# A gated feed-forward after windowed attention: w_gate's products in block form too, with PSUM banks taken in pairs

## The chip, the core and the metric

The kernel runs on one core of one Trainium2 chip. A core has a matrix engine (TensorE, here PE, with its weight loads PEld), three engines for everything else (VectorE or DVE, ScalarE or ACT, GpSimd or POOL), a queue that issues DMAs (SyncE or SP; POOL issues DMAs too), an on-chip memory SBUF and the accumulators PSUM, eight banks of 128 partitions by 512 float32. Each engine runs its instructions in order and waits on semaphores for the others. The metric is the device time of one execution in microseconds (us). Three timed runs of the kernel before gave 322.5, 322.76 and 321.5; the median is 322.5.

## The reference

Inputs are q, k, v of (8 batches, 8 heads, 576 positions, 64), and three weight matrices; everything is given as float32.

```python
scores = scale * q @ k.T            # only the 64 last positions of each query count
attn   = softmax(scores) ; x = (attn @ v) as (4608 tokens, 512)
gate   = maximum(x @ w_gate, 0)     # 512 x 1536
val    = x @ w_val                  # 512 x 1536
out    = (gate * val) @ w_out       # 1536 x 512
```

## The kernel before, in words

The tokens are cut into ten tiles: four narrow ones of 384 tokens (tiles 0 to 3) and six wide ones of 512 (tiles 4 to 9). For each tile x is made transposed in SBUF (`xt`: 512 features as 4 blocks of 128 partitions, by tokens), then a stage called hidden makes `g_sb = relu(x w_gate) * (x w_val)`, 12 blocks of 128 columns, and a stage called output multiplies it by w_out, 128 tokens at a time, copies each result from PSUM (`o_sb`, on ACT) and stores it (SP). Everything in the matmuls is float16, the accumulation float32.

Attention for later tiles is woven into these stages. `scores` (wide) and `u_st` (narrow) compute scores into PSUM, ACT takes exp, DVE masks; `values` multiplies by v, DVE divides by the sums (L436, L441) and transposes the result into `xt` (L447). q and k come by DMA (L173, issued by POOL, one buffer for each of four halves) and are transposed by DVE (L193, 1.24 us each, 32 in all); v comes by DMA (L199) and is spread to a second place by POOL (`v_spread`, L208 and L210).

**Order.** `W`, the Weaver, keeps a planned clock and a heap of due times. PE's instructions are emitted in the order of the code; each emission first pops all other work whose due time has come, so the order on every engine is fixed when the program is built. `W.pop()` in a loop emits work early until something (a free bank, a sum) is there. `plan_batch` plans the loads and transposes of one batch of q and k, `qk_ahead` gives it the time of the load (12 us ahead of T) and of the four transposes; `v_ahead` does it for v.

**Banks.** `singles` are eight PSUM tiles of one bank each. In the narrow tiles `one_bank` goes round the first four and `two_banks` round the other four. From the first wide tile on, `free` lists banks not in use; `bank()` takes the oldest, and the reader of a bank appends it again.

**Hidden of a narrow tile** (`hidden`, L507 to L545): in sets of four blocks, first the four products with w_gate, each into a bank, with a relu by ACT into one slot of `r4` (L522), then four with w_val, each multiplied by its relu by DVE straight from PSUM into `g_sb` (L525).

**Hidden of a wide tile** (`fast_hidden`, L547 to L642): three groups. Each covers two blocks of the first half of the columns and two of the second. w_val's part is done with seven products of half-size blocks instead of eight (a Strassen-like scheme). P1 to P7 are products of sums of weight blocks (`vs`, made once by POOL in `w_form`, L480) with differences of x blocks (`xc`, four for each tile, made by DVE in `x_form`, L459). P1, P6, P7 and P4 run up in one bank, A: after P1, P6 and P7 ACT copies the running sum out (`snap`, L593), and the next product is added on top. P2 goes to bank B; P5 and P3 to bank C. DVE adds B or C to a copy (L600), and POOL multiplies that sum by its relu into `g_sb` (L606); the last one, P4's, DVE multiplies straight from PSUM (`direct`, L613). Between these products stand the four full products with w_gate (`gate`, 4 matmuls of 512 columns each, L582), each with a relu by ACT from PSUM (L586).

**Output of a wide tile** (`fast_output`): four rows of 128 tokens, 12 matmuls of 512 columns each (L658); ahead of the first two stand the values of the next tile, ahead of the last two the scores of the one after.

Of the kernel before, what the change touches and what calls it, by code (L numbers as in the profile page):

```python
# [15 lines left out]
SUB = mybir.AluOpType.subtract  # L16
ONE_ONE = struct.unpack("<f", struct.pack("<I", 0x3C003C00))[0]
# [29 lines left out]
def kernel(  # L47
# [23 lines left out]
    WT = 512  # L71
# [15 lines left out]
    singles = [psum.tile([128, 512], FP32, name=f"bank{i}") for i in range(8)]  # L87
# [7 lines left out]
    vs = persist.tile([128, 4, 2, 128 * HF], FP16)  # L95
    qTs = [persist.tile([128, 2, S, 2], FP16, name=f"qT{i}") for i in range(2)]
# [266 lines left out]

    def bank():

        while not free:
            W.pop()
        return free.pop(0)
# [83 lines left out]
    def x_form(t, n):  # L452

        if t not in xcs:
            xcs[t] = x_sb.tile([128, 4, 2, HT], FP16, name="xc", tag="xt")
        xt, xc = xt_tile(t), xcs[t]
        b11, b12, b21, b22 = (xt[:, 2 * k:2 * k + 2, HT * h:HT * h + HT] for k in range(2) for h in range(2))
        x, y = ((b12, b11), (b22, xc[:, 0]), (b22, b12), (b21, xc[:, 1]))[n]
        nc.vector.tensor_tensor(xc[:, n], x, y, SUB)  # L459
        if n == 3:  # L460
            normed[0] = t

    def values(t, hh, T, banks=None):
# [7 lines left out]
        for n in ((0,), (1, 2, 3))[hh]:  # L471
            W.at(T + 4.0 + 0.4 * n, lambda n=n: x_form(t, n))

    def w_form(n, j):

        c = slice(256 * j, 256 * j + 256)
        f = slice(256 * j + 128 * HF, 256 * j + 128 * HF + 256)
        a11, a12, a21, a22 = wv[:, 0:2, c], wv[:, 2:4, c], wv[:, 0:2, f], wv[:, 2:4, f]
        x, y, op = ((a21, a22, ADD), (vs[:, 0, :, c], a11, SUB), (a11, a21, SUB), (a12, vs[:, 1, :, c], SUB))[n]
        nc.gpsimd.tensor_tensor(vs[:, n, :, c], x, y, op)  # L480
# [26 lines left out]
    def hidden(t, spans, f0=0, f1=NF, each=1):  # L507
# [20 lines left out]
        for fb in range(f0, f1, each):  # L528
            r4 = f_sb.tile([128, 4, WT], FP32, name="r4", bufs=2)
            r_sbs = {}  # L530
            for i, wt in enumerate((wg, wv)):
                for c0, f in ((c0, f) for c0, _ in spans for f in range(fb, fb + each, w)):
# [8 lines left out]
                    if i == 0:  # L541
                        r_sb = r_sbs[c0, f] = r4[:, len(r_sbs)]
# [4 lines left out]
    def fast_hidden(t):  # L547
# [3 lines left out]
        b11, b12, b21, b22 = (xt[:, 2 * k:2 * k + 2, HT * h:HT * h + HT] for k in range(2) for h in range(2))  # L551
        halves = lambda ap: ap.rearrange("p f (h n) -> p f h n", h=2)
        pair = lambda ap: ap.rearrange("p (f n) -> p f n", f=2)

        def group(j):
            c = slice(256 * j, 256 * j + 256)
            f = slice(256 * j + 128 * HF, 256 * j + 128 * HF + 256)
            r4 = f_sb.tile([128, 4, WT], FP32, name="r4", bufs=2)
            rh = halves(r4)
            gh = halves(g_sb)  # L560
            at = {}
            forms = {"P1": (wv[:, 0:2, c], b11), "P2": (wv[:, 2:4, c], b21), "P3": (vs[:, 3, :, c], b22),
                     "P4": (wv[:, 2:4, f], xc[:, 3]), "P5": (vs[:, 0, :, c], xc[:, 0]),
                     "P6": (vs[:, 1, :, c], xc[:, 1]), "P7": (vs[:, 2, :, c], xc[:, 2])}

            def product(name, to, first):
                W.advance(W.clock)
                if first:
                    at[to] = bank()
                w, x = forms[name]  # L570
                for i in range(2):
                    for k in range(2):
                        nc.tensor.matmul(at[to][:, HT * i:HT * i + HT], w[:, k, 128 * i:128 * i + 128], x[:, k],  # L573
                                         start=(first and i == 0 and k == 0), stop=(k == 1), skip_group_check=True)
                W.clock += 4 * (HT + 7) / 2400.0

            def gate(n):
                W.advance(W.clock)
                to = bank()
                ff = 2 * j + n % 2 + HF * (n // 2)  # L580
                for k in range(NC):
                    nc.tensor.matmul(to, wg[:, k, 128 * ff:128 * ff + 128], xt[:, k], start=(k == 0), stop=(k == NC - 1))  # L582
                W.clock += 4 * (WT + 7) / 2400.0

                def relu():
                    nc.scalar.activation(r4[:, n], to, ACT.Relu)  # L586
                    free.append(to)
                W.at(W.clock, relu)

            def snap(name):  # L590
                def copy():
                    at[name] = f_sb.tile([128, 512], FP32, name="snap", bufs=5)
                    nc.scalar.copy(at[name], at["A"])  # L593
                W.at(W.clock, copy)

            def add(delay, to, name, last, n, h):

                def summed():
                    v = f_sb.tile([128, 512], FP32, name="vsum", bufs=4)
                    nc.vector.tensor_tensor(v, at[to], at[name], ADD)  # L600
                    at["summed", n, h] = True
                    if last:
                        free.append(at[to])

                    def mult():
                        nc.gpsimd.tensor_tensor(gh[:, 2 * j + HF * n:2 * j + HF * n + 2, h], rh[:, 2 * n:2 * n + 2, h], pair(v), MUL)  # L606
                        done[2 * j + HF * n, h] = done[2 * j + HF * n + 1, h] = True
                    W.at(max(W.clock, at["relus", n]) + 0.7, mult)
                W.at(W.clock + delay, summed)

            def direct():
                def mult():
                    nc.vector.tensor_tensor(gh[:, 2 * j + HF:2 * j + HF + 2, 0], rh[:, 2:4, 0], pair(at["A"]), MUL)  # L613
                    free.append(at["A"])
                    done[2 * j + HF, 0] = done[2 * j + HF + 1, 0] = True
                W.at(W.clock + 0.2, mult)

            T = W.clock
            at["relus", 1], at["relus", 0] = T + 3.7, T + 6.8
            product("P1", "A", True)  # L620
            snap("a1")
            gate(2)
            product("P6", "A", False)
            snap("u2")
            product("P2", "B", True)
            add(0.1, "B", "a1", True, 0, 0)
            gate(3)
            product("P5", "C", True)
            product("P7", "A", False)
            snap("u3")  # L630
            add(0.8, "C", "u3", False, 1, 1)
            gate(0)
            product("P4", "A", False)
            direct()
            gate(1)
            while ("summed", 1, 1) not in at:
                W.pop()
            product("P3", "C", False)
            add(0.1, "C", "u2", True, 0, 1)

        for j in range(NF // 4):
            group(j)  # L642
# [76 lines left out]
    with tc.manual_schedule():  # L719
# [115 lines left out]
        def qk_ahead(t, T, gaps):  # L835
            b, new = batch_of(t)
            if new:
                plan_batch(b, T - 12.0, [T + x for x in gaps])
# [13 lines left out]
        def ahead(t):  # L852
# [3 lines left out]
            if t == NS - 2:  # L856
                qk_ahead(NS, T + 20.5, (0.0, 1.5, 3.0, 4.5))
                v_ahead(NS, T + 27.0)
                for j in range(NF // 4):
                    for n, at in enumerate((0, 1, 3, 2)):  # L860
                        W.at(T + 12.0 + 6.4 * j + 1.6 * n, lambda at=at, j=j: w_form(at, j))
            if t == NS - 1:
# [9 lines left out]
                qk_ahead(NS + 2, T + 27.6, SLOTS)  # L872
# [7 lines left out]
        W.at(15.0, lambda: loads(3, 70.0))  # L880
        T = 67.0
# [65 lines left out]
```

## Time and profile before

| | |
|---|---|
| timed runs, median (range) | 322.5 us (321.5 to 322.76) |
| profiled execution, span from first to last instruction | 320.2 us |
| mean granted PE clock | 0.995 |
| one wide tile, hidden and output (223.09 to 256.0) | 32.9 us, of which hidden 19.6 |
| busy in a wide tile's hidden stage without q/k transposes (256.0 to 275.5): PE, DVE, ACT, POOL | 19.5, 7.4, 12.3, 8.6 us |
| the same with four q/k transposes (190.2 to 209.7) | 19.5, 12.0, 12.3, 13.0 us |

No time of the profiled execution as a whole is recorded besides its span; the timed runs lie 1.3 to 2.6 us above it. In the rows of the profile, "x" is a count, "busy, mean ns" the time of a group and of one instruction, and after the bar stands the idle time of the engine just before them and what ended it. A matmul's row gives a modelled end, which includes the way through the array; matmuls that follow each other start earlier than the row before ends.

### The profile page before, as it was taken

To read this page: it belongs to the slowest core of one execution; us is meant where nothing else is said; L and a number is where in the kernel's file an instruction comes from. 1 tells how busy PE (TensorE), PEld (TensorE's weight loads), DVE (VectorE), ACT (ScalarE), POOL (GpSimd) and SP (SyncE) were. 2 spreads that over 40 slices of the span, in tenths; PEclk is the share of its full clock that TensorE was granted. 3 is DMA by queue.
4 is the path that set the end of the run, shared out by engine and by line. 5 is a ranking of instruction groups with operands and counts; after the bars stand their busy time and mean duration, and the time that the engine had idled before them with its cause. 6 is when DMAs were issued, how large, how long until landed. Compare 5 with 4: busy or idle time off the path is not lost.

```text
span 320.2 us, 9481 instructions
## 1 busy us (share of the span) xinstructions
PE 308.8 (96%) x4077; PEld 190.1 (59%) x4077; DVE 203.2 (63%) x397; ACT 158.1 (49%) x310; POOL 177.8 (56%) x206
## 2 busy tenths in 40 slices
PE   4799999999899999999999999999999999999996
PEld 2586958655546555665566556655665566546654
DVE  6937962667993996779576857686337734643420
ACT  3644325533524616752765276627652666326632
POOL 8859336215988506799168925980495036404540
PEclk9889999999999999999999999999999999999999
DMA  8999998946299149806910691039001100020002
GB/s 218 183 196 205 194 120 161 171 98 99 30 174 165 21 90 160 57 1 104 219 36 0 97 220 43 2 50 127 35 0 34 69 34 3 2 98 35 0 33 102
DMA packets 52491, 29.52 MB, mean 92 GB/s; under 512 B 38880, under 2 KB 43872, under 8 KB 52448
## 3 DMA queue, kind: packets, MB, share of 16 engines
q0 software_dynamic: 46688, 18.29, 49.3%
q1 hardware_dynamic: 5616, 10.55, 9.3%
q8 instruction: 32, 0.52, 0.7%
q14 instruction: 11, 0.09, 0.1%
q10 hardware_dynamic: 144, 0.07, 0.1%
HBM read 37.75 MB, written 9.44 MB: 147 GB/s over the span
## 4 chain that ended last, share of the span: by engine, by line
PE 89%; DVE 3%; ACT 2%; POOL 2%; DMA 2%; issue 1%; DVEq 0%; POOLq 0%
PE bank L658 19%; PE bank L582 19%; PE bank L538 17%; PE bank L573 17%; PE bank L673 10%; PE bank L253 3%; PE bank L422 2%; DVE p L292 2%; DMA v<-in_v_dram 2%; ACT pw L389 1%; PE bank L311 1%; DVE g_sb L525 1%; PE bank L703 1%; POOL v L199 1%; DVE qT L193 0%
## 5 line engine op out<-in xcount | busy, mean ns | idle before, releaser
L606 POOL TENSOR_TENSOR g_sb<-r,vsum 128x512 f16<-128x512 f32 x54 | 68.1, 1276 | 77.7 <-DVE vsum L600 75.7
L600 DVE TENSOR_TENSOR vsum<-bank,snap 128x512 f32<-128x512 f32 x54 | 37.3, 691 | 60.1 <-PE bank L573 36.5
L582 PE MATMUL bank<-xt,wg 128*128 128x512 f16 x288 | 73.9, 379 | 0.0
L658 PE MATMUL bank<-wo,g_sb 128*128 128x512 f16 x276 | 62.9, 380 | 0.0
L586 ACT ACTIVATE r<-bank 128x512 f32<-128x512 f32 x72 | 43.2, 600 | 32.3 <-PE bank L582 32.3
L658 PEld LDWEIGHTS <-g_sb 128*128 128x128 f16 x276 | 25.5, 98 | 28.9
L582 PEld LDWEIGHTS <-wg 128*128 128x128 f16 x288 | 28.2, 98 | 18.6
L525 DVE TENSOR_TENSOR g_sb<-r,bank 128x384 f16<-128x384 f32 x48 | 25.9, 550 | 20.3 <-PE bank L538 18.8
L522 ACT ACTIVATE r<-bank 128x384 f32<-128x384 f32 x48 | 23.7, 496 | 29.4 <-PE bank L538 20.3
L573 PEld LDWEIGHTS <-vs 128*128 128x128 f16 x288 | 28.0, 98 | 15.6 <-issue 1.6
L538 PE MATMUL bank<-xt,wg 128*128 128x192 f16 (+1 forms) x256 | 36.5, 296 | 0.5 <-DVE g_sb L525 0.4
L663 ACT COPY o_sb<-bank 128x512 f32<-128x512 f32 x23 | 13.5, 586 | 45.2 <-PE bank L658 43.2
L593 ACT COPY snap<-bank 128x512 f32<-128x512 f32 x54 | 31.6, 586 | 8.4 <-PE bank L573 8.4
L199 POOL DMA_DIRECT2D v<-in_v_dram x41 | 34.7, 865 | 1.8 <-DMA q<-in_q_dram 1.0
L538 PE MATMUL bank<-xt,wv 128*128 128x192 f16 (+1 forms) x256 | 34.3, 286 | 0.0
L673 PE MATMUL bank<-wo,g_sb 128*128 128x512 f16 x144 | 32.8, 379 | 0.2 <-DVE g_sb L525 0.2
L538 PEld LDWEIGHTS <-wg 128*128 128x128 f16 x256 | 24.3, 102 | 9.8 <-issue 0.9
L573 PE MATMUL bank<-xc,vs 128*128 128x256 f16 x216 | 29.4, 272 | 0.4 <-ACT snap L593 0.4
L208 POOL COPY v<-v 64x512 f16<-64x512 f16 (+1 forms) x22 | 16.1, 732 | 23.7 <-DMA v<-in_v_dram 22.6
L538 PEld LDWEIGHTS <-wv 128*128 128x128 f16 x256 | 22.9, 98 | 8.1
L394 DVE TENSOR_TENSOR pw<-pw,mask 128x512 f16<-128x512 f16 x48 | 20.2, 437 | 11.2 <-ACT pw L389 10.5
L389 ACT ACTIVATE pw<-bank 128x512 f16<-128x512 f32 x48 | 25.9, 608 | 1.5 <-PE bank L253 1.0
(69 smaller groups left out, 358.6 us busy)
## 6 DMA issues: line engine op xcount, KB each, us to landing
out_dram<-o_sb SPq DMA_DIRECT2D x35, 256.0 KB, 3.0
k<-in_k_dram POOLq DMA_DIRECT2D x15, 288.0 KB, 5.3
q<-in_q_dram POOLq DMA_DIRECT2D x15, 288.0 KB, 7.3
v<-in_v_dram POOLq DMA_DIRECT2D x31, 128.0 KB, 8.0
wg<-in_moe_w_gate_dram POOLq DMA_DIRECT2D x6, 256.0 KB, 6.4
wv<-in_moe_w_val_dram POOLq DMA_DIRECT2D x6, 256.0 KB, 8.2
wo<-in_moe_w_out_dram POOLq DMA_DIRECT2D x3, 512.0 KB, 11.9
v<-in_v_dram POOLq DMA_DIRECT2D x10, 64.0 KB, 5.9
```

What stands on the lines that cost most here:

```text
L199: nc.gpsimd.dma_start(v16s[b % 2][lo:hi, g, :, 0:64], v[b, :, 64 * g - 64 + lo:64 * g - 64 + hi].rearrange("h p d -> p h d"))
L389: nc.scalar.activation(d["p"][g].rearrange("p n c -> p (n c)"), d["st"][g], ACT.Exp, scale=scale)
L525: nc.vector.tensor_tensor(g_sb[:, f:f + w, c0:c0 + n], part(r_sb), part(h2), MUL)
L538: nc.tensor.matmul(h[:, b * n:b * n + n], wt[:, c, (f + b) * 128:(f + b) * 128 + 128], xt[:, c, c0:c0 + n], start=(c == 0), stop=(c == NC ...
L573: nc.tensor.matmul(at[to][:, HT * i:HT * i + HT], w[:, k, 128 * i:128 * i + 128], x[:, k], start=(first and i == 0 and k == 0), stop=(k == ...
L582: nc.tensor.matmul(to, wg[:, k, 128 * ff:128 * ff + 128], xt[:, k], start=(k == 0), stop=(k == NC - 1))
L586: nc.scalar.activation(r4[:, n], to, ACT.Relu)
L593: nc.scalar.copy(at[name], at["A"])
L600: nc.vector.tensor_tensor(v, at[to], at[name], ADD)
L606: nc.gpsimd.tensor_tensor(gh[:, 2 * j + HF * n:2 * j + HF * n + 2, h], rh[:, 2 * n:2 * n + 2, h], pair(v), MUL)
L658: nc.tensor.matmul(op, g_sb[:, f, 128 * sub:128 * sub + 128], wo[:, f], start=(i == 0), stop=(i == NF - 1))
L673: nc.tensor.matmul(op, g_sb[:, f, bass.ds(sub * 128, 128)], wo[:, f], start=(f == 0), stop=(f == NF - 1))
```

## The change: w_gate also in seven block products

The six wide tiles compute w_gate's part in the same seven-product form as w_val's. The two run side by side: each product is emitted for w_gate (i = 0) and then for w_val (i = 1). Bank A becomes two banks, one for each, B and C become pairs of neighbouring banks. The eight PSUM tiles are declared as four tiles of two banks, and `singles` are views of their halves. The copies of A go into the two halves of an SBUF tile `pr`; one DVE addition over 1024 columns adds both banks of B (or of C, the second time) to it; after P7 there are two additions of 512, since C goes on being used. ACT then takes the relu of the gate half in SBUF, and POOL multiplies the two halves. `bank()` prefers a bank whose neighbour is in use, and `bank_pair()` takes two neighbours. The first product of the next group is put between P4 and P3. POOL makes weight sums `us` of w_gate, 12 more instructions, planned from 42 us on; three of the four x differences of each tile go from DVE to POOL. One batch of q and k is loaded 6 us before its time instead of 12. The narrow tiles keep their computation; they use the new bank views, and `pr` pairs in place of `r4`.

```diff
-    singles = [psum.tile([128, 512], FP32, name=f"bank{i}") for i in range(8)]
+    pairs = [psum.tile([128, 2, 512], FP32, name=f"bank{i}") for i in range(4)]
+    singles = [pairs[i // 2][:, i % 2] for i in range(8)]
...
+    us = persist.tile([128, 4, 2, 128 * HF], FP16)
...
     def bank():
         while not free:
             W.pop()
-        return free.pop(0)
+        return take(next((to for to in free if not is_free(partner(to))), free[0]))
+
+    def bank_pair():
+        while True:
+            for to in free:
+                if is_free(partner(to)):
+                    i = next(i for i in range(8) if singles[i] is to) // 2
+                    return pairs[i], [take(singles[2 * i]), take(singles[2 * i + 1])]
+            W.pop()
...
-        nc.vector.tensor_tensor(xc[:, n], x, y, SUB)
+        (nc.vector if n == 1 else nc.gpsimd).tensor_tensor(xc[:, n], x, y, SUB)
...
-        for n in ((0,), (1, 2, 3))[hh]:
-            W.at(T + 4.0 + 0.4 * n, lambda n=n: x_form(t, n))
+        for n, x in (((0, 4.0),), ((1, 4.0), (2, 4.1), (3, 5.0)))[hh]:
+            W.at(T + x, lambda n=n: x_form(t, n))
...
-            r4 = f_sb.tile([128, 4, WT], FP32, name="r4", bufs=2)
+            r2s = [f_sb.tile([128, 2, WT], FP32, name="pr", bufs=6) for _ in range(2)]
...
+        TO = {"P1": "A", "P6": "A", "P7": "A", "P4": "A", "P2": "B", "P5": "C", "P3": "C"}
+        AFTER = {"P6": ("P1", "snap"), "P7": ("P6", "snap"), "P4": ("P7", "snap"), "P3": ("P7", "sum")}
+
+        def product(j, name, i):
+            W.advance(W.clock)
+            if name in AFTER:
+                before, what = AFTER[name]
+                while (j, what, before, i) not in at:
+                    W.pop()
+            first = name in ("P1", "P2", "P5")
+            if name == "P1":
+                at[j, "A", i] = bank()
+            elif first and i == 0:
+                at[j, TO[name]], (at[j, TO[name], 0], at[j, TO[name], 1]) = bank_pair()
+            to = at[j, TO[name], i]
+            w, x = operands(name, *kinds[i], j)
+            for m in range(2):
+                for k in range(2):
+                    nc.tensor.matmul(to[:, HT * m:HT * m + HT], w[:, k, 128 * m:128 * m + 128], x[:, k],
+                                     start=(first and m == 0 and k == 0), stop=(k == 1), skip_group_check=True)
+            W.clock += 4 * (HT + 7) / 2400.0
...
+            def copy():                                   # in snap(j, name, i)
+                nc.scalar.copy(pr[:, i], at[j, "A", i])
...
+            def relu():                                   # in finish(j, name, n, h)
+                nc.scalar.activation(pr[:, 0], pr[:, 0], ACT.Relu)
+            def mult():
+                nc.gpsimd.tensor_tensor(gh[:, f:f + 2, h], pair(pr[:, 0]), pair(pr[:, 1]), MUL)
...
+                if i is None:                             # in add(...)
+                    flat = [ap.rearrange("p a n -> p (a n)") for ap in (at[j, bank_name], pr)]
+                    nc.vector.tensor_tensor(flat[1], flat[0], flat[1], ADD)
+                    free.extend(at[j, bank_name, m] for m in range(2))
+                else:
+                    nc.vector.tensor_tensor(pr[:, i], at[j, bank_name, i], pr[:, i], ADD)
...
+        step(0, "P1")
+        for j in range(last + 1):
+            for name in ("P2", "P6", "P5", "P7") if j == 0 else ("P6", "P2", "P7", "P5"):
+                step(j, name)
+            tail = [(j, "P4"), (j + 1, "P1"), (j, "P3")] if j else [(j + 1, "P1"), (j, "P4"), (j, "P3")]
+            for jj, name in tail:
+                if jj <= last:
+                    step(jj, name)
...
-                qk_ahead(NS + 2, T + 27.6, SLOTS)
+                qk_ahead(NS + 2, T + 27.6, SLOTS, 6.0)
...
+        for j in range(NF // 4):
+            for n, at in enumerate((0, 1, 3, 2)):
+                W.at(42.0 + 8.8 * j + 2.2 * n, lambda at=at, j=j: w_form(wg, at, j))
```

In `step`, each of the two products of a name is followed by its `snap` (P1, P6, P7), and the additions, the relu of P4's gate bank and DVE's direct multiply are planned behind them as before.

## The prediction

> **What bounds the kernel now.** I read the page's first two parts, then the chain that ended last, then the costliest groups, then the timeline of one wide tile.
>
> ```profile
> span 320.2 us, 9481 instructions
> PE 308.8 (96%) x4077; PEld 190.1 (59%) x4077; DVE 203.2 (63%) x397; ACT 158.1 (49%) x310; POOL 177.8 (56%) x206
> ...
> PE 89%; DVE 3%; ACT 2%; POOL 2%; DMA 2%; issue 1%; DVEq 0%; POOLq 0%
> ...
> L582 PE MATMUL bank<-xt,wg 128*128 128x512 f16 x288 | 73.9, 379 | 0.0
> L586 ACT ACTIVATE r<-bank 128x512 f32<-128x512 f32 x72 | 43.2, 600 | 32.3 <-PE bank L582 32.3
> L525 DVE TENSOR_TENSOR g_sb<-r,bank 128x384 f16<-128x384 f32 x48 | 25.9, 550 | 20.3 <-PE bank L538 18.8
> L522 ACT ACTIVATE r<-bank 128x384 f32<-128x384 f32 x48 | 23.7, 496 | 29.4 <-PE bank L538 20.3
> L593 ACT COPY snap<-bank 128x512 f32<-128x512 f32 x54 | 31.6, 586 | 8.4 <-PE bank L573 8.4
> ```
>
> PE is busy for 96% and carries 89% of the chain. Its matmul groups have 0.0 to 0.5 us of idle time ahead of them; ACT and DVE idle, and PE is what releases them. So time falls only with PE's issue time, and grows with each wait put in front of PE. The timeline of the fourth wide tile shows how those waits stand today (start, length, engine, line).
>
> ```profile
> 223.03 0.49 PE L573 MATMUL bank<-xt,wv 128*128 128x256 f16 x3
> 223.16 0.59 ACT L663 COPY o_sb<-bank 128x512 f32<-128x512 f32 x1 [0.66 <-ACT pw L389]
> ...
> 223.65 0.59 ACT L593 COPY snap<-bank 128x512 f32<-128x512 f32 x1
> ...
> 224.29 0.60 PE L573 MATMUL bank<-xc,vs 128*128 128x256 f16 x4
> ...
> 226.02 1.04 PE L573 MATMUL bank<-xc,vs 128*128 128x256 f16 x8
> ...
> 226.90 1.03 PE L582 MATMUL bank<-xt,wg 128*128 128x512 f16 x4
> 227.10 0.59 ACT L593 COPY snap<-bank 128x512 f32<-128x512 f32 x1 [0.28 <-PE bank L573]
> ...
> 227.78 0.69 DVE L600 TENSOR_TENSOR vsum<-bank,snap 128x512 f32<-128x512 f32 x1 [1.63 <-ACT snap L593]
> ```
>
> Eight 256-column matmuls start at 226.02 and PE's next group at 226.90 (0.108 us each, so a block product of four issues in 0.433). Their modelled end is 227.06, 0.17 after the issue ends; the copy starts 0.04 later. The copy of 223.65 ends at 224.24 and the product that waited for it starts at 224.29, 0.05 later. Now a 0.86 us gate product lies in that gap; the wait costs 0.07.
>
> **The change, part by part.**
>
> *The products.* A group of a wide tile has 16 matmuls of 512 columns (0.216 us: four in 0.86, "226.90" to the next) and 28 of 256; after, 56 of 256. 16 x 0.216 + 28 x 0.108 = 6.49, against 56 x 0.108 = 6.07. That is 0.42 less, 1.27 for a tile's three groups, 7.6 for six tiles, if nothing waits.
>
> *The banks.* PSUM's eight tiles of one bank become four of two banks, and all code, narrow tiles too, uses halves of them. In the built program I counted out whose completion each PE wait names. P6 with wv writes the second half of a pair, and its wait is not for the copy of its own half. It is for the copy of the *other* half, which was issued just after P6 with wg:
>
> ```
> L606 Matmult bank1_83<-xc_2922,us_90 128x256 [waits Activation_49]   P6, wg: waits for the copy of P1's wv half
> L606 Matmult bank1_83<-xc_2922,vs_89 128x256 [waits Activation_49]   P6, wv: waits for the copy of P6's wg half
> ```
>
> So a pair is guarded as one tile: whoever writes a half waits for the last reader of either. With the products of w_gate and w_val alternating in the two halves of pair A, the wv product always waits out a full round trip that the wg product has just begun; and PE, in order, holds everything behind it (its own other products, and through them ACT and DVE, which idle).
>
> Price of a round trip: 0.17 drain + 0.05 + reader + 0.05. Reader 0.59 (a copy): 0.86. Relu of 384 (0.496): 0.76. Gate multiply of 384 (0.55): 0.82. Bounds: 0.76 for the first if the copy counts with its back-to-back spacing (o_sb at 223.16, snap at 223.65: 0.49), 0.96 if ACT is late by another 0.1.
>
> Wide tile, from the list of waits:
> - P1, P6, P7, P4 with wv, three groups: 12 x 0.86 = 10.3. A wait for the wg copy stands at each; P4's is for the relu.
> - The tile's first P1 takes the other half of the pair that held the last output row: 0.86 for the copy to o_sb.
> - The third group's P1 pair is the second group's P4 pair. DVE's direct multiply reads its wv half and is itself put behind P1 with wg, and the copy of that P1 behind the multiply: 0.17 + 0.05 + 0.69 + 0.05 + 0.59 + 0.05 = 1.60 instead of 0.86: 0.75 more.
>
> 12.0, less 1.3 for the products: hidden goes from 19.6 (223.09 to 242.69) to 30.3. Six tiles: **+64**.
>
> Narrow tiles: 24 bank fills each, 96 in all. Every second fill is the second half of its pair; the list shows 24 of them behind the relu of the half filled just before and 22 behind its gate multiply: 24 x 0.76 + 22 x 0.82 = **+36**. Before, each fill had a bank of its own, and L538's groups waited 0.5 and 0.0.
>
> Output rows: a row in the half beside the row before waits for its copy to o_sb. With two narrow fills that do the same these are 11 x 0.86 = 9.5; two first rows wait for a gate multiply, 1.6. In five wide tiles the first output row shares a pair with a values bank and waits for DVE to normalise it, some 0.9 each, 4.7 (0 if DVE is early, 1.4 each if its queue is full). **+16**, less some 1 us of PE waits of before that are contained in these.
>
> *The other edits, hidden.* ACT gets three operations more per group (six copies, four relus, against three and four): 54 x 0.6 = 32 us. With 6.07 us of PE per group it would be tight (10 starts of 0.49); with 10.3 it is covered by PE's own waits. DVE: two sums of 1024 and two of 512 for three of 512. No row has 1024 from PSUM; L525 to L600 grows 0.141 us in 128 columns, so 0.69 + 0.56 = 1.25, bounds 1.1 (no second fixed part) and 1.38 (two of 512): +1.8 a group, 33 us, less 18 differences at 0.42 to 0.52. Behind those sums wait the relus, the products P3 and the GpSimd multiplies; all have over 1 us of slack in a group of 10. Without that cover see rival C. GpSimd: 12 weight sums at 1.16 (L480's rows) and 18 differences, nearest row the same, 1.2. The first five weight sums lie in its idle stretch before 45.4 (9.7 us); three stand ahead of the k/q DMA issues of 48.4 and delay them by 3.6, three more ahead of the v issues of 50.5 (7.2 in all), one in the idle 8.8 before 62.05. The k/q transposes start at 66.65 and the v copies are wanted at 86, so landing times of 5.3 to 8.0 leave room. The differences stand behind the four k/q loads and ahead of the v loads; they end before the next tile's P6, since some 9 us of output rows lie between. The four loads issued 6 us later still land (5.3 and 7.3) before their transposes. All 0; ends -1 and +3.
>
> Sum: 64 + 36 + 15 = +115. The profiled execution's span is 320.2, the median of the timed runs 322.5, 2.3 around it; so a span of 435.5, and **438**.
>
> **A rule weighed.** The Trainium skill ("PSUM — Partial Sum Buffer", PSUM bank collisions) asks for guards by bank, and says different banks don't collide; by it the waits between halves are needless and the sum would be rival C's. The built program has them all the same, and it is what runs.
>
> **Rivals.**
>
> *B, the clock falls as well.* The granted clock was 0.63 from 13.8 to 18.4 us, right after 5.5 us in which PE was busy for only 3.86, and 1.00 once PE had run without gaps:
>
> ```profile
> 8.30:13.80 5.50, 3.86 (x196) 2.56 (x196) 5.12 (x12) 3.78 (x16) 3.93 (x7) 1.00 1.71 175
> 13.80:18.40 4.60, 4.46 (x34) 4.05 (x33) 2.23 (x6) 2.69 (x9) 4.60 (x7) 0.63 1.24 204
> 18.40:22.40 4.00, 4.00 (x43) 3.48 (x42) 2.22 (x4) 1.00 (x3) 1.65 (x3) 1.00 1.53 191
> ```
>
> After the change PE issues for some 60% of a wide hidden stage and 63% of a narrow one. At 0.63 the narrow ones' 96 x 0.64 (four matmuls of 384; sixteen took 2.76) = 61 us of issue grow by 36 (474), the wide ones' 6 x 18.2 by another 64 (538). Against it: that stretch was the start, with products of 64 columns; no gap now would exceed 1.9 us. The Trainium skill ("TensorE: Matmul & The Clock Gate", Part 1: The HAM clock gate) has the clock fall after an idle window of some 3.4 us, by which it would hold here; no row shows a warm PE with such gaps.
>
> *C, halves guarded apart.* Then copies end 0.44 us before their next product (0.43 + 0.17 + 0.05 + 0.59 + 0.05 = 1.29 of 1.73). What remains per tile is 0.43 for the first P1 and 0.74 for the third group's P1 behind relu and direct multiply, against 1.34 gained: -0.2. In the three tiles with q/k transposes (1.24 each) among DVE's sums, the direct multiply comes 1.5 later and P3 0.8: +2.2. 3 x 2.2 - 3 x 0.2 = +6: 328. Against it stands the counted list.
>
> *D, not slower.* As C, and DVE's transposes fall into its idle time: 322.5 - 7.6 = 315, up to 322. One wait decides: PE's for the wg half's copy at the wv product. It would have to be under 0.11 us (7.6 over the 72 of them); the round trip is 0.86.
>
> **How the numbers follow.** As worked out 0.72, B 0.20, C 0.05, D 0.03. The likeliest's own range: about 150 waits at 0.1 less or more, 424 to 453. The range must take in half of B: 424 to 500. Less than 0.5% (1.6 us) can't be told from no change here: faster 0.02, same 0.01, slower 0.97.
>
> **What would show it.** PE's busy share falls to some 70%, and PE leads the list of waits: on ACT's copies some 50 us, on ACT's and DVE's work of the narrow tiles 18 each, on the wide relu 15. A wide hidden stage lasts 30 us, its wv products start 0.86 after the wg product's issue ended. PEclk stays 9 (B: falls to 6). Copies at L617 idle before them for PE, not the reverse. Wrong if a wide tile's hidden stage stays under 25, or if PE's idle time before L562 is small.

## The result

The changed kernel takes 441.04 us (median of 4 runs, 439.74 to 443.1), the kernel before 322.0 (321.46 to 322.76): a ratio of 1.370, 95% interval 1.365 to 1.374. It is 119 us slower, where +115 and 438 were predicted. The profiled execution's span is 438.4 us at a granted clock of 0.992, against 320.2 at 0.995.

The page of the kernel after: span and busy times, the rows of TensorE and its clock by slices, the chain that ended last, and three of the costliest groups.

```profile
span 438.4 us, 9997 instructions
PE 324.0 (74%) x4293; PEld 211.1 (48%) x4293; DVE 240.3 (55%) x397; ACT 187.3 (43%) x364; POOL 213.0 (49%) x236
...
PE   5667687876787687669766886688668866886686
...
PEclk9899999999999999999999999999999998999999
...
PE 64%; ACT 18%; DVE 10%; issue 4%; DMA 1%; POOL 1%; ACTq 0%; DVEq 0%; POOLq 0%
...
L617 ACT COPY pr<-bank 128x512 f32<-128x512 f32 x108 | 62.8, 586 | 71.2 <-PE bank L606 62.1
L643 DVE TENSOR_TENSOR pr<-bank,pr 128x1024 f32<-128x1024 f32 x36 | 44.1, 1224 | 51.2 <-PE bank L606 50.1
...
L606 PE MATMUL bank<-xc,vs 128*128 128x256 f16 x216 | 32.3, 271 | 26.2 <-ACT pr L617 26.2
```

No engine is full any more: PE fell from 96% to 74%, and every other engine stands at 55% or less. The chain is shared by PE (64%), ACT (18%) and DVE (10%), where PE alone had 89%. PE idles for ACT's copy (26.2 us ahead of one of its groups), and ACT's copy idles for PE (62.1 us). Two engines that wait for each other in turn: that is what a round trip looks like in the groups. PEclk shows an 8 in two slices, one at the start and one at 362 to 373 us; a slice is 11 us long, and what happened in the second stands below.

The list of waits of PE, after (us in total, times, longest):

```profile
PE bank L606 <- ACT pr L617: 45.4, 54, 1.6
PE bank L562 <- DVE g_sb L549: 15.4, 22, 1.4
PE bank L562 <- ACT pr L546: 13.8, 21, 1.3
PE bank L606 <- ACT r L656: 12.6, 18, 0.7
...
PE bank L723 <- ACT o_sb L730: 3.5, 5, 0.7
PE bank L708 <- DVE xw L464: 3.4, 5, 1.0
PE bank L606 <- ACT o_sb L713: 2.9, 4, 0.7
PE bank L708 <- ACT o_sb L713: 2.7, 4, 0.7
PE bank L723 <- DVE g_sb L549: 1.7, 2, 1.1
PE bank L562 <- ACT o_sb L730: 1.4, 2, 0.7
```

The first and the fourth line are the wide tiles: 54 waits for the copies of P1, P6 and P7 (three of each in six tiles) and 18 for the relu of P4. The second and third are the narrow tiles, the rest rows of output and their neighbours. PE's idle time is counted from the modelled end of a matmul, so 0.17 us for the drain has to be added to each.

The timeline of PE in the second wide tile, after (start, length, engine, line, and in brackets the idle time before and its releaser):

```profile
213.17 0.60 PE L606 MATMUL bank<-xt,wg 128*128 128x256 f16 x4 [0.72 <-ACT o_sb L713]
214.50 0.60 PE L606 MATMUL bank<-xt,wv 128*128 128x256 f16 x4 [0.73 <-ACT pr L617]
...
215.80 0.60 PE L606 MATMUL bank<-xc,us 128*128 128x256 f16 x4
217.13 0.60 PE L606 MATMUL bank<-xc,vs 128*128 128x256 f16 x4 [0.73 <-ACT pr L617]
...
231.59 0.60 PE L606 MATMUL bank<-xt,wg 128*128 128x256 f16 x4
233.84 0.60 PE L606 MATMUL bank<-xt,wv 128*128 128x256 f16 x4 [1.65 <-ACT pr L617]
```

P1 with w_gate, P1 with w_val, P6 with w_gate, P6 with w_val start at 213.17, 214.50, 215.80 and 217.13: one step in 1.30 to 1.33 us, of which the product itself issues for 0.43. What lies between is 0.90: 0.17 of drain, 0.09 until the copy starts (213.86), 0.58 of copy, 0.06 until PE goes on. The last two lines are the third group's P1: 1.65 idle, 2.25 from start to start. The next row of the timeline that isn't hidden work is at 243.10, so the stage lasts 29.9 us, and 30.8 with the 0.89 that PE stood before it.

The fifth wide stage takes 31.1 us, 1.3 more than the fourth. In it the granted clock fell to half. First two stretches (from and to, length, busy time and instructions of PE, PEld, DVE, ACT and POOL, granted clock, DMA share, GB/s), then two products in the second stretch:

```profile
364.97:368.38 3.41, 1.45 (x12) 1.15 (x12) 1.40 (x3) 1.49 (x3) 2.21 (x2) 1.00 0.00 0
368.38:371.79 3.41, 2.79 (x14) 1.83 (x13) 1.23 (x1) 1.11 (x2) 0.00 (x0) 0.50 0.00 0
```

```profile
368.40 1.06 PE L606 MATMUL bank<-xt,us 128*128 128x256 f16 x4
369.26 1.06 PE L606 MATMUL bank<-xt,vs 128*128 128x256 f16 x4
```

Products start 0.85 us apart there instead of 0.43, three of them, and that is the 1.3 us. In the 3.41 us before the fall PE was busy for 1.45; its longest single idle time was 1.52 us, the wait of the third group's P1.

Where the 118.2 us of span came from, by the stages of the two traces (hidden with the values that are woven into it):

| stage | before | after | difference |
|---|---|---|---|
| start to the first wide product (narrow tiles) | 122.3 | 166.2 | +44.0 |
| six wide hidden stages | 119.9 | 182.2 | +62.3 |
| output rows after them, with scores and values | 78.0 | 90.0 | +12.0 |

### The profile page after: what moved, and what is told of

It is laid out like the page before. It is cut to its first block, busy times and chain, and to the rows that moved or that the text cites. A ratio compares the mean times of both kernels' runs of the same rounds, so it can differ in the third digit from the quotient of the medians.

```text
span 438.4 us, 9997 instructions
## 1 busy us (share of the span) xinstructions
PE 324.0 (74%) x4293; PEld 211.1 (48%) x4293; DVE 240.3 (55%) x397; ACT 187.3 (43%) x364; POOL 213.0 (49%) x236
## 4 chain that ended last, share of the span: by engine, by line
PE 64%; ACT 18%; DVE 10%; issue 4%; DMA 1%; POOL 1%; ACTq 0%; DVEq 0%; POOLq 0%
PE bank L606 26%; PE bank L562 14%; PE bank L708 13%; ACT pr L617 9%; PE bank L723 7%; DVE g_sb L549 4%; ACT pr L546 3%; PE bank L256 2%; ACT r L656 2%; PE bank L445 2%; ACT pw L412 1%; DMA v<-in_v_dram 1%; DVE p L295 1%; ACT o_sb L730 1%; ACT o_sb L713 1%
## 5 line engine op out<-in xcount | busy, mean ns | idle before, releaser
L630 POOL TENSOR_TENSOR g_sb<-pr 128x512 f16<-128x512 f32 x54 | 68.5, 1270 | 118.2 <-ACT pr L627 117.3
L617 ACT COPY pr<-bank 128x512 f32<-128x512 f32 x108 | 62.8, 586 | 71.2 <-PE bank L606 62.1
L643 DVE TENSOR_TENSOR pr<-bank,pr 128x1024 f32<-128x1024 f32 x36 | 44.1, 1224 | 51.2 <-PE bank L606 50.1
L549 DVE TENSOR_TENSOR g_sb<-pr,bank 128x384 f16<-128x384 f32 x48 | 26.5, 552 | 51.4 <-PE bank L562 50.9
L606 PE MATMUL bank<-xc,vs 128*128 128x256 f16 x216 | 32.3, 271 | 26.2 <-ACT pr L617 26.2
L546 ACT ACTIVATE pr<-bank 128x384 f32<-128x384 f32 x48 | 23.6, 492 | 58.6 <-PE bank L562 53.4
L627 ACT ACTIVATE pr<-pr 128x512 f32<-128x512 f32 x54 | 34.1, 631 | 15.0 <-DVE pr L643 11.8
L646 DVE TENSOR_TENSOR pr<-bank,pr 128x512 f32<-128x512 f32 x36 | 23.8, 687 | 27.3 <-PE bank L606 14.8
L562 PEld LDWEIGHTS <-wg 128*128 128x128 f16 x256 | 24.1, 100 | 27.8 <-issue 19.9
L723 PE MATMUL bank<-wo,g_sb 128*128 128x512 f16 x144 | 33.6, 379 | 5.2 <-ACT o_sb L730 3.5
L606 PE MATMUL bank<-xt,wv 128*128 128x256 f16 x144 | 21.6, 272 | 19.2 <-ACT pr L617 19.2
L606 PE MATMUL bank<-xc,us 128*128 128x256 f16 x216 | 32.9, 275 | 0.0
```

Source lines behind the costliest of these rows:

```text
L546: nc.scalar.activation(part(r_sb), part(h1), ACT.Relu)
L549: nc.vector.tensor_tensor(g_sb[:, f:f + w, c0:c0 + n], part(r_sb), part(h2), MUL)
L562: nc.tensor.matmul(h[:, b * n:b * n + n], wt[:, c, (f + b) * 128:(f + b) * 128 + 128], xt[:, c, c0:c0 + n], start=(c == 0), stop=(c == NC ...
L606: nc.tensor.matmul(to[:, HT * m:HT * m + HT], w[:, k, 128 * m:128 * m + 128], x[:, k], start=(first and m == 0 and k == 0), stop=(k == 1), ...
L617: nc.scalar.copy(pr[:, i], at[j, "A", i])
L627: nc.scalar.activation(pr[:, 0], pr[:, 0], ACT.Relu)
```

## The experiments

The theory: the two halves of a bank pair are guarded as one tile, and this alone makes the kernel slower. Its rivals: the seven-product form itself (more sums, more copies), the work moved to GpSimd, the order of the products, and the 1024-wide sums.

### Each bank its own tile again

Everything else of the change stays. The sums over two banks become two of 512 each.

```diff
-    pairs = [psum.tile([128, 2, 512], FP32, name=f"bank{i}") for i in range(4)]
-    singles = [pairs[i // 2][:, i % 2] for i in range(8)]
+    singles = [psum.tile([128, 512], FP32, name=f"bank{i}") for i in range(8)]
...
-                    flat = [ap.rearrange("p a n -> p (a n)") for ap in (at[j, bank_name], pr)]
-                    nc.vector.tensor_tensor(flat[1], flat[0], flat[1], ADD)
+                    for m in range(2):
+                        nc.vector.tensor_tensor(pr[:, m], at[j, bank_name, m], pr[:, m], ADD)
```

> The kernel after with eight PSUM tiles of one bank again; B and C still take neighbouring banks, but each pair sum of 1024 columns becomes two sums of 512. All products, copies, relus, differences and weight sums stay. Theory (the guard on a pair of banks is the cost): the 46 waits of the narrow tiles and the 72 of the wide tiles' second halves go, and rival C's price is left, 328 us (324 to 334): per wide tile the third group's P1 still waits some 0.7 us behind relu and direct multiply of P4, and the three tiles with q/k transposes lose some 2 us each to them. Rival (ACT's three more operations per group and DVE's more sums are the cost, or fourteen alternating products are slow by themselves): stays over 400 us, since none of these is taken away.

Measured: 326.52 us, 1.0135 of before (1.0112 to 1.0158). 114.5 of the 119 us are gone with the declaration and the split sums (that the sums aren't the cost is shown below, where they stay whole). The busy times on its page, and then PE's waits in it:

```profile
PE 304.5 (94%) x4293; PEld 209.7 (65%) x4293; DVE 238.3 (73%) x433; ACT 182.7 (56%) x364; POOL 213.5 (66%) x236
```

```profile
PE bank L605 <- DVE g_sb L664: 4.4, 3, 1.5
...
PE bank L605 <- ACT r L655: 1.7, 6, 0.4
PE bank L605 <- ACT o_sb L712: 1.1, 4, 0.3
```

PE is full again. The kernel is 4.5 us slower than before, though its products issue in 7.6 us less. The largest waits left in the wide tiles are three of up to 1.5 us, one in each wide tile that has q and k transposes. The timeline of PE at one of them, and that of DVE:

```profile
171.49 0.60 PE L605 MATMUL bank<-xt,wg 128*128 128x256 f16 x4 [0.25 <-ACT r L655]
173.58 0.60 PE L605 MATMUL bank<-xt,wv 128*128 128x256 f16 x4 [1.50 <-DVE g_sb L664]
```

```profile
171.19 1.23 DVE L195 STREAM_TRANSPOSE qT<-q 128x576 f32<-128x576 f32 x1
172.26 0.68 DVE L645 TENSOR_TENSOR pr<-bank,pr 128x512 f32<-128x512 f32 x1
172.86 0.67 DVE L664 TENSOR_TENSOR g_sb<-r,bank 128x512 f16<-128x512 f32 x1
```

The third group's P1 with w_val goes into the bank that the direct multiply still has to read; that multiply stands behind a transpose of 1.23 us and a sum, starts at 172.86 and ends at 173.53, and PE starts at 173.58. The hidden stages of the six tiles changed by +2.2, +1.6, +1.6, -0.1, -0.1 and -0.6 us against before. This is rival C of the prediction, with its place, its mechanism and nearly its size (328 forecast, +2.2 for a tile with transposes).

### Bank pairs alone, in the kernel before

```diff
-    singles = [psum.tile([128, 512], FP32, name=f"bank{i}") for i in range(8)]
+    pairs = [psum.tile([128, 2, 512], FP32, name=f"bank{i}") for i in range(4)]
+    singles = [pairs[i // 2][:, i % 2] for i in range(8)]
```

> The kernel before with one edit: its eight PSUM tiles are declared as four of two banks, and the single banks are their halves. No instruction is added or moved. Theory: every use of a half waits for the last reader of the other. The narrow tiles cost the same +36 us as in the kernel after (24 waits on a relu at 0.76, 22 on a gate multiply at 0.82), narrow output rows and fills some +8; in the wide tiles A, B, C and the gate banks are now neighbours by chance, and the list of waits shows some 34 round trips in hidden (+27) and some in the output rows (+12): 405 us (390 to 418). Rival (the cost belongs to the doubled products of w_gate): near 322 us.

Measured: 409.75 us, 1.271 (1.267 to 1.275). PE's waits in it:

```profile
PE bank L539 <- DVE g_sb L526: 15.4, 22, 1.4
PE bank L539 <- ACT r L523: 13.7, 21, 1.3
PE bank L574 <- ACT r L587: 11.0, 19, 0.8
PE bank L583 <- ACT snap L594: 7.2, 11, 1.2
```

No operation was added, no size changed, and 88 us came. The two lines of the narrow tiles (L539) are those of the kernel after, to 0.1 us and to the count. The rest lies in the output rows and in the wide tiles, whose hidden stages take 24.1 to 25.0 us against 19.7 from the second tile on. So the declaration alone makes a kernel slower by 27%, with none of the other edits.

### The edits on other engines alone

The kernel before, with three of four x differences on GpSimd, twelve weight sums on GpSimd that nothing uses, and the later load of one batch of q and k.

```diff
-        nc.vector.tensor_tensor(xc[:, n], x, y, SUB)
+        (nc.vector if n == 1 else nc.gpsimd).tensor_tensor(xc[:, n], x, y, SUB)
...
-                qk_ahead(NS + 2, T + 27.6, SLOTS)
+                qk_ahead(NS + 2, T + 27.6, SLOTS, 6.0)
...
+        for j in range(NF // 4):
+            for n, at in enumerate((0, 1, 3, 2)):
+                W.at(42.0 + 8.8 * j + 2.2 * n, lambda at=at, j=j: w_form(wg, at, j))
```

> The kernel before with the side edits alone: three of four x differences on GpSimd, twelve weight sums of w_gate on GpSimd (made and not used), and the one q/k load at 6 us ahead. It computes what the kernel before computes. Theory: all of it hidden, 322 us (320.5 to 325). Rival (GpSimd's queue delays loads, spreads or differences that PE waits for): 326 us or more, with PE waits on GpSimd's differences or on spread v.

Measured: 321.89 us, 0.9993 (0.9979 to 1.0007). The interval takes in 1: no cost of these edits shows, as the prediction had it.

### The products in another order

The changed kernel, with the two halves of a product further apart: P6 and P2 of w_gate, then P6 and P2 of w_val, and P7 and P5 likewise.

```diff
-        def step(j, name):
-            for i in range(2):
-                product(j, name, i)
+        def step(j, *names):
+            for name, i in ((name, i) for i in range(2) for name in names):
+                product(j, name, i)
...
-            for name in ("P2", "P6", "P5", "P7") if j == 0 else ("P6", "P2", "P7", "P5"):
-                step(j, name)
+            for names in (("P2", "P6"), ("P5", "P7")) if j == 0 else (("P6", "P2"), ("P7", "P5")):
+                step(j, *names)
```

> The kernel after with another order on PE: P6 and P2, P7 and P5 are emitted in turns (P6 w_gate, P2 w_gate, P6 w_val, P2 w_val), so that a product of 0.43 us lies between the two halves of pair A. Theory: pair A is a chain of round trips in series, 2 x (0.43 + 0.86) = 2.59 us per name whatever lies between, and the 0.87 us of P2 or P5 fills it in either order: 441 us (436 to 445), with about twice as many waits of half the size. Rival (the loss is that w_val's product stands right behind w_gate's): 36 of the 72 waits are halved, 426 us or less.

Measured: 442.61 us, 1.374 (1.371 to 1.378). The wait for the copies, in the list of PE's waits:

```profile
PE bank L606 <- ACT pr L617: 36.3, 76, 1.8
```

There are 76 of these waits, 36.3 us together, where the changed kernel has 54 with 45.4: more and shorter ones, though not twice as many of half the size. The hidden stages don't get shorter; they take 29.7 to 31.9 us from the second tile on, and 33.6 in the first. P6 with w_gate and P6 with w_val in the third tile:

```profile
263.55 0.60 PE L606 MATMUL bank<-xc,us 128*128 128x256 f16 x4 [0.24 <-ACT pr L617]
...
264.88 0.60 PE L606 MATMUL bank<-xc,vs 128*128 128x256 f16 x4 [0.29 <-ACT pr L617]
```

The two still start 1.33 us apart, with another product between them. Putting 0.43 us of other work between the halves doesn't help, since the wait at one half isn't the limit: product, copy, product, copy of the two halves of A is one serial chain with a step of 1.3 us. Other products fit into it, and can't shorten it. (The 31.9 us holds a stretch at half clock, as above.)

### Pairs only where pairs are summed

The changed kernel with four banks as tiles of their own and two pairs. P1, P6, P7 and P4 run up in single banks; B and C are pairs and keep their sums over 1024 columns. Whoever else needs one bank takes the oldest, half of a pair or not.

```diff
-    pairs = [psum.tile([128, 2, 512], FP32, name=f"bank{i}") for i in range(4)]
-    singles = [pairs[i // 2][:, i % 2] for i in range(8)]
+    pairs = [None, None] + [psum.tile([128, 2, 512], FP32, name=f"pair{i}") for i in range(2)]
+    singles = [psum.tile([128, 512], FP32, name=f"bank{i}") for i in range(4)] + [pairs[i // 2][:, i % 2] for i in range(4, 8)]
...
-        return take(next((to for to in free if not is_free(partner(to))), free[0]))
+        return take(free[0])
...
-                at[j, "A", i] = bank()
+                at[j, "A", i] = bank_of_a()
```

> The changed kernel with four of the eight banks declared as tiles of their own (all narrow products, output rows, q, k and the wide products that are summed first go there, oldest free bank first) and four as two tiles of two banks, which the four differences' sums keep for their 1024-wide additions. Theory (a bank pair that is one tile is guarded as one, and this alone made the 119 us): only the wide hidden stages pay, since there alone are pairs written; two pairs serve six products in turns, so a pair's two halves still wait for copy and addition of each other. A wide hidden stage with 12 of the 18 pair round trips spread over two pairs that alternate costs at most 12 x 0.86 = 10 us more per tile in the worst case (60 us in all), and with the pair's reader overlapped by the other pair's products some 1 to 2 us (6 to 12 us in all): 328 to 340 us. Rival: the 1024-wide sums themselves (1.22 us each, twice as long as one over a single bank) are the cost, wherever the other products are; then the wide stage keeps the 30.7 us that it takes in the changed kernel against 19.6 before, and the time is 322 + 6 x 11 = 388 us or more.

Measured: 338.04 us, 1.0495 (1.0459 to 1.0530), within the theory's 328 to 340, far from the rival's 388. In the timeline of PE of this kernel a wide tile starts so, with P1 and then P2:

```profile
236.47 0.60 PE L614 MATMUL bank<-xt,wg 128*128 128x256 f16 x4
236.91 0.60 PE L614 MATMUL bank<-xt,wv 128*128 128x256 f16 x4
237.34 0.60 PE L614 MATMUL pair<-xt,wg 128*128 128x256 f16 x4
237.78 0.60 PE L614 MATMUL pair<-xt,wv 128*128 128x256 f16 x4
```

The second line, P1 with w_val, starts 0.44 us after the first; in the changed kernel it waited 0.73 for the copy (at 214.50). The third and fourth line write the two halves of one pair, also 0.44 us apart, as they did in the changed kernel (214.93 and 215.37). The sum that reads them comes after both and reads both, so guarding them as one adds no wait. The hidden stages of the last three tiles take 19.1 to 19.2 us, less than before's 19.6 to 19.7, with the 1024-wide sums in them. So neither these sums nor pairs as such are the cost. Against the single-bank kernel with the same bank rule (318.69 us, next) this one is 19 us slower. Most of that it pays where a half has a reader of its own:

```profile
PE pair L614 <- DVE pr L654: 6.0, 8, 1.1
PE pair L716 <- DVE xw L472: 5.9, 10, 0.6
...
PE pair L256 <- ACT pw L420: 2.8, 3, 1.3
```

These readers are the sums of 512 after P7 (L654), and those of the values and scores of the attention that were given a half of a pair (L472, L420). In the first wide tile, amid three such waits of 1.3 us, the granted clock is also 0.50 from 126.4 to 133.2 us.

### The oldest bank first, transposes moved, differences back on DVE

Three kernels on the first experiment's, to see what its 4.5 us are and whether the seven products can pay. The first takes the bank that has been free longest; the second also moves the four slots of the q and k transposes and sets the planned length of a wide hidden stage (`L_T`) to 18.41 us in place of 19.59; the third has, instead of that, all x differences on DVE.

```diff
-        return take(next((to for to in free if not is_free(partner(to))), free[0]))
+        return take(free[0])
```

> The single-bank version that took 326.5 us, with one more edit: a product that needs one bank takes the bank that has been free longest, and no longer first the one whose neighbour is in use. Theory: there, the third group's first product landed in banks that the direct gate multiply (behind a q or k transpose of 1.24 us on VectorE) had still to read; these three waits of 1.5 us (4.4 us in all) and the short ones on ScalarE's relu and output rows (1.7 and 1.1 us) go. 326.5 - 4.4 to 326.5 - 7.2: 319.5 to 322.5 us, so no slower than before. Rival: TensorE then meets the next thing that is late (VectorE is 73% busy and has 36 more sums than before), the waits move one product on, and the time stays within 1 us of 326.5.

```diff
-        L_T = 3 * 6.53
+        L_T = 18.41
...
-        SLOTS = (2.6, 6.53 + 0.8, 6.53 + 2.6, 2 * 6.53 + 0.8)
+        SLOTS = (4.0, 6.0, 10.5, 12.5)
```

> As the single-bank version with the oldest bank first, and the slots of the q and k transposes (VectorE, 1.24 us each) in the wide tile moved by 1 to 2 us of the planner's time, away from the direct gate multiplies. Theory: what waits on the direct multiplies are left goes, 0.5 to 1.5 us against the kernel without the move: 318.5 to 322 us. Rival: the multiplies are no longer on the path once the banks are taken oldest first, and the two kernels are the same within 0.3 us.

```diff
-        (nc.vector if n == 1 else nc.gpsimd).tensor_tensor(xc[:, n], x, y, SUB)
+        nc.vector.tensor_tensor(xc[:, n], x, y, SUB)
```

> As the single-bank version with the oldest bank first, with all x differences on VectorE again (18 move from GpSimd). Theory: beside GpSimd's differences a VectorE difference took 1.27 us, alone 0.42; so VectorE pays 18 x 0.42 = 7.6 us for these, saves 6 x 0.85 = 5.1 us on its own six and some 0.05 to 0.1 us on each of 48 masks (2 to 5 us), and its busy time stays about where it was; the time is within 0.5 us of the version with GpSimd's differences. The difference rows should fall from 1.27 to 0.42 and the masks from 0.53 to 0.44. Rival: VectorE carries the late work of the wide stage, and 18 more operations there cost up to 18 x 0.42 = 7.6 us: up to 329 us.

Measured, against before: 318.69 us (0.9890, 0.9867 to 0.9913) with the oldest bank first, 318.17 (0.9873, 0.9846 to 0.9899) with the transposes moved too, 319.44 (0.9917, 0.9893 to 0.9940) with the differences on DVE. All three take 0.8 to 1.3% less time than the kernel before, with intervals below 1. The first lies a little below the range of its theory (319.5 to 322.5), the second a little below its own (318.5 to 322). The third is 0.75 us slower than the first where at most 0.5 was expected, and far from its rival's 329. The waits on the direct multiply and on the relu are gone from the first one's list. The busy times on its page, and the longest of PE's waits in its wide tiles, now for sums:

```profile
PE 301.9 (95%) x4293; PEld 209.7 (66%) x4293; DVE 238.9 (75%) x433; ACT 181.2 (57%) x364; POOL 213.1 (67%) x236
```

```profile
PE bank L605 <- DVE pr L645: 1.4, 4, 0.4
```

Moved and unmoved transposes can't be told apart by the time, whose intervals overlap. The stages can: the second and third tile fell from 19.4 to 18.7 and 18.5 us, and the first rose from 22.3 to 23.4. So one more kernel, with the old slots in the first wide tile and the moved ones after it:

```diff
-                qk_ahead(NS + 2, T + 27.6, SLOTS, 6.0)
+                qk_ahead(NS + 2, T + 27.6, (2.6, 7.33, 9.13, 13.86), 6.0)
```

> As the single-bank version with the oldest bank first; the q and k transposes stand in their old slots in the first wide tile and in the moved slots in the second and third. From the two runs before it: the first wide tile's hidden stage took 22.3 us with the old slots and 23.4 with the moved ones, the second and third 19.4 each with the old and 18.7 and 18.5 with the moved. Theory (what is left of the seven-product gain is lost only behind VectorE's transposes): the stages add, so the first takes 22.3, the others 18.4 to 18.7, and the time is 318.7 - 1.6 = 317.1 us, 316.5 to 317.8. Rival: a transpose that is moved out of one stage is late for the scores behind it, and gives the gain back between the stages: 318.2 to 318.7 us.

Measured: 317.08 us (316.39 to 317.25), 0.9837 of before (0.9823 to 0.9850), 317.1 expected. The hidden stages in the traces, us:

| wide tile | 1 | 2 | 3 | 4 | 5 | 6 |
|---|---|---|---|---|---|---|
| before | 21.5 | 19.7 | 19.7 | 19.7 | 19.7 | 19.6 |
| changed | 31.6 | 29.9 | 29.9 | 29.8 | 31.1 | 29.8 |
| single banks | 23.7 | 21.3 | 21.3 | 19.6 | 19.6 | 19.0 |
| and the oldest first | 22.3 | 19.4 | 19.4 | 18.4 | 18.4 | 18.3 |
| and two sets of slots | 22.3 | 18.7 | 18.5 | 18.4 | 18.4 | 18.3 |

In the tiles without transposes the whole 1.27 us of the products arrives. In the first tile it doesn't: it takes 0.8 us more than before. The trace shows PE's waits there (P6 at 125.55 for a copy, 0.38 us; the next group's P1 at 129.79 for an exp, 0.30; P3 at 131.47 and 143.86 for DVE's sums, 0.21 and 0.39). The sum ahead of 131.47 stood behind two masks that took 2.31 us together, where a mask's mean is 0.55. What would give the 0.8 us back wasn't tried.

## Why the prediction was right

The table sets the prediction's terms beside the waits of the list, each with 0.17 us of drain added to its idle time.

| term | predicted | from the list of waits after |
|---|---|---|
| wide tiles | 12.0 x 6 - 7.6 = 64 | 45.4 + 12.6 + 2.9 + 76 x 0.17 - 7.6 = 66 |
| narrow tiles | 36 | 15.4 + 13.8 + 43 x 0.17 = 36.5 |
| output rows | 16 - 1 | 3.5 + 3.4 + 2.7 + 1.7 + 1.4 + 18 x 0.17 = 15.8 |
| sum | 115 | 118, the spans differ by 118.2 |

The rows differ from the table of stages since narrow tiles have output rows too, and since a wide tile's first wait lies ahead of its stage.

*The guard.* That a pair is guarded as one tile was read from the built program, and its cost is now shown in both directions: put into the kernel before it costs 88 us, taken out of the changed kernel it gives 114.5 back. That last step also split the sums in two; with whole sums, and pairs for nothing but B and C and whoever was handed a half, the time is 338. The counts of waits were 54 + 18 in the wide tiles, and 24 and 22 predicted against 21 and 22 in the narrow ones.

*The round trip.* 0.86 predicted, 0.90 measured: the copy starts 0.09 after the modelled end, not 0.05. Over 72 waits that is 2.9 us, about the whole miss of the sum; smaller ones cancel. The third group's P1 was to cost 0.75 over a plain round trip; it shows 1.65 of idle in the tiles with transposes and 1.52 in the others against 0.73, so 0.92 and 0.79. Of the six first products that were to wait for an output row, four did (1.7 us less), and the 1.3 us at half clock stands in no term. That the sum lands within 1% owes something to this cancelling; the large terms, 64 and 36, were each met within 3 us.

*The products.* 1.27 us a tile can't be seen in the changed kernel, since its chain and not PE's issue sets the pace. With single banks and the oldest bank first it is 19.70 - 18.43 = 1.27 in the fourth and fifth tile.

*The edits put down as hidden.* Those on GpSimd and the load came to 0.9993 of before when made alone. DVE's sum of 1024 took 1.224 us (1.25 estimated). ACT's busy time grew by 29 us (32 estimated) and DVE's by 37, where 33 less some 8 for the differences was worked out; of the missing 12, 5 are the x differences that became slower and 3.5 the masks (see the last section); the remaining 3.5 weren't traced.

*The rivals.* B, the clock, came once and in small: 0.50 for 3.41 us, 1.3 us of time, where B had 36 to 100; over the run the clock is 0.992. The prediction had no row of a warm PE with such gaps, and this is one. The Trainium skill ("TensorE: Matmul & The Clock Gate", Part 1: The HAM clock gate) has the clock fall after an idle window of some 3.4 us; here PE's idle times in the 3.41 us before the fall were 1.52 us and less, and it was busy for 1.45 of them. So the page's window doesn't rule out B, as the prediction took it to. C and D, halves guarded apart, were right as descriptions of another program: the 326.5 us of single banks are C's waits in C's tiles, and 317 to 319 lie in D's range once the bank order lets the direct multiply's bank rest.

*The rule weighed.* What the Trainium skill asks for ("PSUM — Partial Sum Buffer", PSUM bank collisions) is a guard by bank; single-bank tiles give just that, and the changed kernel took 114.5 us less with them than with guards by pair. The page told what is needed, the built program told what is paid.

## What to carry to other kernels

A tile that spans two PSUM banks was waited for as a whole in these kernels: declare it so only where each of its readers reads all of it after all its writes, and count the waits in the built program before trusting that two halves are independent. A view that saves one instruction (two sums of 0.68 us became one of 1.22) can put a round trip of 0.9 us into every accumulation. Where banks are handed out, try the one that has been free longest, above all when its last reader stands behind long work on a shared engine: that was worth 7.8 us here, and turned a loss of 1.3% into a gain of 1.1%.

## What the runs showed of the hardware

DVE's x differences took three times as long as before, though neither their shape nor their operands changed. The same group by line and form, in the kernel before, with the side edits alone, and with the oldest bank first but all differences on DVE:

```profile
L459 DVE TENSOR_TENSOR xc<-xt,xc 128x512 f16<-128x512 f16 x12 | 5.1, 422 | 0.2
```

```profile
L460 DVE TENSOR_TENSOR xc<-xt,xc 128x512 f16<-128x512 f16 x6 | 7.6, 1272 | 0.5
```

```profile
L481 DVE TENSOR_TENSOR xc<-xt,xc 128x512 f16<-128x512 f16 x12 | 5.0, 421 | 0.2
L416 DVE TENSOR_TENSOR pw<-pw,mask 128x512 f16<-128x512 f16 x48 | 20.4, 441 | 11.8 <-ACT pw L411 11.0
```

It is 0.42 us where GpSimd makes no differences and 1.27 where it does; the masks go from 437 ns before to 532 with GpSimd's differences and back to 441 without. The timeline of one tile, with GpSimd's differences (single banks, the oldest first):

```profile
151.86 2.31 POOL L481 TENSOR_TENSOR xc<-xt 128x512 f16<-128x512 f16 x2
153.10 1.36 DVE L481 TENSOR_TENSOR xc<-xt,xc 128x512 f16<-128x512 f16 x1 [0.34 <-POOL xc L481]
```

DVE's difference starts at 153.10, as the second of GpSimd's two starts, which ends at 154.17, and DVE's ends at 154.46, 0.3 after it. It looks as if it had waited GpSimd's out and then run at nearly its usual 0.42; had both run at half speed, it would have taken some 0.84. The Trainium skill says so of a VectorE operation with two inputs in SBUF beside a GpSimd operation that reads SBUF: one has the shared pair of ports for its whole instruction, and the other is blocked ("SBUF — State Buffer", SBUF: two separate sides). The runs agree with it in these numbers, but GpSimd's spans are rough, and no run here tried the two apart by themselves. It cost no time that shows: the kernels with and without GpSimd's differences take 318.69 and 319.44 us. DVE's sums from PSUM didn't change with it (680 and 681 ns).

TensorE's clock fell to 0.50 four times in the middle of a profiled execution, for 3.4 or 6.8 us, each time after 3.41 us with little work on PE: 1.45 us busy in the changed kernel (at 368.4), 1.08 and 1.25 with the products in another order (at 189.5 and 281.7), 0.87 with pairs only where pairs are summed (at 126.4). After 1.71 of 3.41 us (changed kernel, 320.59 to 324.00) and after 1.59 (pairs alone in the kernel before, 167.09 to 170.50) it stayed at 1.00. Near the start of the kernel before it fell after 2.36 of 3.41 us (10.91 to 14.32), mostly in products of 64 and 65 columns, so PE's busy time alone doesn't tell when it falls. No run here varied the gaps on purpose.
